# One decode block on one core: maxima by VectorE transposes, softmax sums at the end, wo in 512 columns, and w2 on 112 partitions

## The chip, the core and the metric

The kernel runs on one core of a Trainium2 chip. A core has a matrix engine (TensorE, PE in the profile; its weight loads are listed as PEld), a vector engine (VectorE, DVE), an activation engine (ScalarE, ACT), a general engine (GpSimd, POOL), a queue engine that here issues nearly all transfers (SyncE, SP), and 16 DMA engines that move data between device memory (DRAM) and the core's on-chip memory (SBUF, 128 partitions). Matrix products land in PSUM. The metric is the device time of one execution in microseconds (us).

## The reference

One decode step of a transformer block: the sum of the input, an attention over a cache, and a feed-forward part, both from the same normalised input.

```python
x = A_x                                   # (4, 1, 512), float32 throughout
xn = _layernorm(x)
# attention: 32 heads of 128, cache of 4096 positions for each of 4 batch rows
q = (xn @ wq).reshape(4, 1, 32, 128).transpose(0, 2, 1, 3)
scores = einsum("bhqd,bhkd->bhqk", q, k_cache) * 128 ** -0.5
o = einsum("bhqk,bhkd->bhqd", softmax(scores), v_cache)
a = o.transpose(0, 2, 1, 3).reshape(4, 1, 4096) @ wo        # wo: (4096, 512)
# feed-forward: w1 (512, 1792), w2 (1792, 512)
f = silu(xn @ w1) @ w2
return x + a + f
```

The two caches are 268 MB each; wq and wo are 8.4 MB each, w1 and w2 3.7 MB each. Every byte of them is read once and used for one query row for each batch row.

## The kernel before, in words

**Tiles.** The work on the caches is cut into T = 32 tiles. Tile i holds G = 4 heads of one batch row; its 4 x 4096 cache rows lie as 128 partitions x 128 rows x 128 numbers, so each head has 32 partitions (PH), and a tile of K or V is 128 partitions x 65,536 bytes. K tiles rotate through two buffers, V tiles through one. `load_tile` (line 72) issues each load from SP's queue.

**One turn of the loop (lines 328 to 349).** For tile i: SP issues the load of K tile i+1. VectorE multiplies K by the query in four steps of 32 rows (`products`, L247), GpSimd adds the halves of each row (L251), VectorE sums what is left (`sums`, L262 and L263) into the scores `s`. `maxima` takes the largest score of each partition (L267), and TensorE turns this column into a row (L269). In the next turn `softmax` takes the maximum over each head's 32 partitions (L275), TensorE spreads the four maxima over all partitions (L279), ScalarE copies them with the factor -scale (L281) and takes the exponentials with it as a bias (L285), summing them by partition into `l`. `values` multiplies the exponentials with the V tile on TensorE (L297, 32 matmuls of 512 columns, in four groups of output partitions that run beside each other) into `o_ps`. `heads_out` adds up `l` over each head's partitions with the matrix `same` (L309), copies `o_ps` out (ScalarE, L311), takes the reciprocal of the sum (L315), puts it into the small weights `w_t` (L316), and adds the scaled result into `o_all` (TensorE, L320).

**Order.** Each engine runs its instructions in the order that the tile framework settles from the program; a buffer's reuse is a wait on the engines that last used it. On SP, the load of V tile i waits until `values(i - 1)` has finished, since there is one V buffer, and the load of K tile i+1 stands in the same queue.

**Start (lines 80 to 223).** x, w1, wq and the first K tile are loaded at once. The normalised x is transposed; the hidden row `hp` is computed in four column blocks of 448 (L179), which lie on partitions 0, 32, 64, 96; silu (L185); its result is transposed by 56 small matmuls of 32-column weights (L191) into `hT`, with FC = 14 columns of 128. Then the queries (L206 to L232).

**Tail (lines 352 to 385).** wo is loaded in two pieces into V's buffer and w2 in four pieces (rows 0 to 6, 7 to 10, 11 to 12, 13 of each partition's 14; `W2_CUTS`) into a K buffer, both on 128 partitions. After the last tile, `o_all` is copied (L367), rearranged (L370, L375), and multiplied with wo and w2: `accumulate` (L135) does four matmuls of 128 columns for one row of weights, one for each block of output columns, all added up in `acc`. Then `acc` is copied out (L382) and stored (L385).

Of the kernel before, what the change touches and what calls it, by code (L numbers as in the profile page):

```python
# [1 line left out]

# [14 lines left out]
POOL_ROWS = 32  # L17
POOL_ROWS_LAST = 16
WO_CUTS = (16,)
W2_CUTS = (7, 11, 13)  # L20


@with_exitstack
def kernel(
# [35 lines left out]
    scale = float(Dh) ** -0.5  # L60
# [22 lines left out]
    FJ = F // 4  # L83
# [8 lines left out]

    ident = const.tile([P, P], F32, name="ident")
    make_identity(nc, ident)
    same = const.tile([P, P], F32, name="same")
    nc.gpsimd.memset(same, 0.0)
    for g in range(G):
        nc.gpsimd.memset(
            same[g * PH : (g + 1) * PH, :].rearrange("p (a g) -> p a g", g=G)[:, :, g], 1.0
        )  # L100
    one = const.tile([1, 1], F32, name="one")
    nc.gpsimd.memset(one, 1.0)
# [19 lines left out]
    o_all = ps_1.tile([H, B, Dh], F32, name="o_all")  # L122
    nc.tensor.matmul(
        o_all.rearrange("h b d -> h (b d)"), w_t[:, 0, :H], p_t.rearrange("p r g -> p (r g)"),
        start=True, stop=False,
    )

    pick = const.tile([P, NR * G], F32, name="pick")
# [2 lines left out]
        ident.rearrange("p (j m) -> p m j", j=4)[:, : NR * G, :],  # L131
        axis=AX, op=ALU.add,
    )

    def accumulate(lhsT, rhs, start=False, stop=False):  # L135

        for j in range(D // P):
            nc.tensor.matmul(  # L138
                acc[32 * j : 32 * j + B, :], lhsT, rhs[:, j * P : (j + 1) * P],
                start=start, stop=stop,  # L140
            )
# [28 lines left out]
    xnT = const.tile([P, DC, B], F32, name="xnT")  # L170
# [3 lines left out]


    hp = ps_s.tile([P, FJ], F32, name="sm")
    for c in range(DC):
        for j in range(4):
            nc.tensor.matmul(  # L179
                hp[32 * j : 32 * j + B, :], xnT[:, c, :], w1_t[:, c, j * FJ : (j + 1) * FJ],  # L180
                start=(c == 0), stop=(c == DC - 1),
            )
    for j in range(4):
        rows = slice(32 * j, 32 * j + B)
        nc.scalar.activation(h_sb[rows, :], hp[rows, :], AF.Silu)  # L185
    ht_ps = ps_s.tile([P, FC, B], F32, name="sm")
    h_f = h_sb.rearrange("b (m f) -> b f m", f=FC)
    for f in range(FC):
        for j in range(4):
            rows = slice(32 * j, 32 * j + B)  # L190
            nc.tensor.matmul(  # L191
                ht_ps[32 * j : 32 * j + 32, f, :], h_f[rows, f, :], ident[rows, rows],
                start=True, stop=True,
            )
    hT = const.tile([P, FC, B], F32, name="hT")
    nc.vector.tensor_copy(hT, ht_ps)


    HJ = H // 4
# [1 line left out]
    for hl in range(HJ):  # L201
        for c in range(DC):
            for j in range(4):
                h = HJ * j + hl
                a = PH - B - B * hl
# [4 lines left out]
                    start=(hl == 0 and c == 0),  # L210
                    stop=(hl == HJ - 1 and c == DC - 1),
# [5 lines left out]
    for b in range(B):  # L217
        nc.tensor.matmul(
            qh_ps[:H, b, :], ident.rearrange("p (h b) -> p b h", b=B)[:, b, :], q_all,
            start=True, stop=True,  # L220
# [1 line left out]
    q_h = const.tile([H, B, Dh], F32, name="q_h")  # L222
    nc.vector.tensor_copy(q_h, qh_ps[:H])

    q_ps, vs, st, ls = {}, {}, {}, {}

    def queries(n):

# [12 lines left out]
    def products(i, a):  # L241

        k, q = ks[i], q_ps[i]
        if a == 0:
            st[i] = small.tile([P, R], F32, name="s")
        z = a + STEP
        nc.vector.tensor_tensor(  # L247
            k[:, a:z, :], k[:, a:z, :], q[:, None, :].to_broadcast([P, STEP, Dh]), op=ALU.mult
        )
# [13 lines left out]
        nc.vector.tensor_reduce(s[:, a:v], k[:, a:v, :half], axis=AX, op=ALU.add)  # L263

    def maxima(i):
        m = small.tile([P, 1], F32, name="m")
        nc.vector.tensor_reduce(m, st[i], axis=AX, op=ALU.max)  # L267
        mt = ps_s.tile([1, P], F32, name="sm")
        nc.tensor.transpose(mt, m, ident)  # L269
        return mt  # L270

    def softmax(i, mt):
        s = st.pop(i)
        gm = small.tile([1, G], F32, name="gm", bufs=1)
        nc.vector.tensor_reduce(  # L275
            gm, mt.rearrange("o (g m) -> o g m", g=G), axis=AX, op=ALU.max
        )
        mb = ps_s.tile([P, G], F32, name="sm")
        nc.tensor.matmul(mb, one.to_broadcast([1, P]), gm, start=True, stop=True)  # L279
        nb = small.tile([P, G], F32, name="nb", bufs=1)  # L280
        nc.scalar.activation(nb, mb, AF.Copy, scale=-scale)  # L281
        l = small.tile([P, 1], F32, name="l_t")
        for g in range(G):
            rows = slice(g * PH, (g + 1) * PH)
            nc.scalar.activation(  # L285
                p_t[rows, :, g], s[rows, :], AF.Exp, bias=nb[rows, g : g + 1], scale=scale,
                accum_out=l[rows, :],
            )
        ls[i] = l

    def values(i):
        v, o = vs.pop(i), o_ps
# [12 lines left out]
    def heads_out(i):  # L305

        h, b = i // B * G, i % B
        lt = ps_s.tile([P, 1], F32, name="sm")
        nc.tensor.matmul(lt, same, ls.pop(i), start=True, stop=True)  # L309
        o_sb = small.tile([P, NR, Dh], F32, name="o_sb", bufs=1)  # L310
        nc.scalar.activation(  # L311
            o_sb.rearrange("p r d -> p (r d)"), o_ps, AF.Copy
        )
        rl = small.tile([P, 1], F32, name="rl", bufs=1)
        nc.vector.reciprocal(rl, lt)  # L315
        nc.vector.tensor_scalar_mul(  # L316
            w_t[:, :, W0 : W0 + G], pick.rearrange("p (r g) -> p r g", r=NR), rl
        )
# [8 lines left out]
    mt = None  # L327
    for i in range(T):
        if i > 0 and i + 1 < T:
            ks[i + 1] = load_tile(kpool, "k_t", k_cache, i + 1)  # L330
        products(i, 0)
        if i > 0:
            softmax(i - 1, mt)
# [11 lines left out]
        mt = maxima(i)  # L345
        if i > 0:
            heads_out(i - 1)
        if i % B == 1 and i + B < T:
            queries(i // B + 1)


    wo_t = vpool.tile([P, R, Dh], F32, name="v_t").rearrange("p (c m) d -> p c (m d)", c=H)
    w2_t = kpool.tile([P, R, Dh], F32, name="k_t").rearrange("p r d -> p (r d)")
    w2_t = w2_t[:, : FC * D].rearrange("p (f n) -> p f n", f=FC)
    for t, w, n, cuts in ((wo_t, wo, H, WO_CUTS), (w2_t, w2, FC, W2_CUTS)):
        w = w.rearrange("(p f) n -> p f n", p=P)
        edges = (0, *cuts, n)
        for a, z in zip(edges[:-1], edges[1:]):
            nc.sync.dma_start(t[:, a:z, :], w[:, a:z, :])  # L359

    softmax(T - 1, mt)
# [12 lines left out]
    ot = const.tile([P, H, B], F32, name="ot")  # L374
    nc.vector.tensor_copy(ot, ot_ps.rearrange("p b c -> p c b"))  # L375
# [42 lines left out]
```

## Time and profile before

| | us |
|---|---|
| Median of 3 runs (1310.25 to 1310.54) | 1310.34 |
| The profiled execution's own time | 1310.07 |
| Its span in the profile | 1308.3 |
| VectorE busy | 911.8 |
| GpSimd busy | 511.0 |
| TensorE busy (weight loads 140.7, beside it) | 401.0 |
| ScalarE busy | 97.6 |

The profile shows one execution. "Busy" is the sum of an engine's instructions; the granted clock is the share of TensorE's full clock that it was given, 0.641 in the mean. An fp32 matmul stands in the records as two passes, each with a weight load. In a view by lines, each row is a group of instructions: line, engine, operation, output and inputs with shapes, how many, then busy us and mean ns of one, then the idle time just before them and what ended it. In a timeline or chain, the first two numbers are the start and the duration in us; "issue" is time in which the engine waited for nothing that the profile shows. A view by windows gives busy time of PE, PEld, DVE, ACT and POOL in a stretch, then the granted clock, the busy share of the 16 DMA engines and the GB/s that they moved. In the DMA issues, the last number is the median us from issue to landing.

### The profile page before, as it was taken

What the parts mean: (1) busy time and instruction counts of PE and PEld (TensorE: products, weight loads), DVE (VectorE), ACT (ScalarE), POOL (GpSimd) and SP (SyncE); (2) the same over time, 40 slices, a digit from 0 to 9 for tenths busy, and PEclk for the clock granted to TensorE, in tenths of its full rate; (3) what the DMA queues carried; (4) which work ended last, traced back from release to release, by engine and by line L of the source; (5) the groups of instructions that cost most, each with busy time, mean ns of one, the idle gap of its engine ahead of it and who ended that gap; (6) DMA issues with size and microseconds to landing.
All of it is one profiled execution on the core that took longest, in us unless ns stands there. A gap on an engine that the chain in (4) does not pass through costs nothing.

```text
span 1308.3 us, 7983 instructions
## 1 busy us (share of the span) xinstructions
PE 401.0 (31%) x3326; PEld 140.7 (11%) x3326; DVE 911.8 (70%) x439; ACT 97.6 (7%) x329; POOL 511.0 (39%) x144
## 2 busy tenths in 40 slices
PE   3412333320333322133332133332033333113337
PEld 1301111100111100011110011110011111001114
DVE  1499666787666787666688666678666678766660
ACT  1010000000000000000000000000000000000000
POOL 0255333444332444332444433344433344433340
PEclk7656666655666656666665566665566666566668
DMA  9999999999999999999999999999999999999997
GB/s 401 444 423 440 427 437 432 433 433 433 438 427 437 429 436 429 437 429 437 432 423 443 421 445 425 439 423 441 429 435 427 436 431 433 433 433 433 435 422 327
DMA packets 10443, 561.51 MB, mean 429 GB/s; under 512 B 1172, under 2 KB 1188, under 8 KB 1448
## 3 DMA queue, kind: packets, MB, share of 16 engines
q1 hardware_dynamic: 10392, 561.01, 99.3%
q8 instruction: 26, 0.43, 0.1%
q14 instruction: 9, 0.07, 0.0%
q10 hardware_dynamic: 16, 0.00, 0.0%
HBM read 561.00 MB, written 0.01 MB: 429 GB/s over the span
## 4 chain that ended last, share of the span: by engine, by line
DMA 65%; PE 19%; DVE 12%; POOL 2%; issue 1%; another core or an unknown queue 0%; SPq 0%; POOLq 0%; DVEq 0%
DMA v_t<-in_A_v_cache_dram 39%; DMA k_t<-in_A_k_cache_dram 22%; PE o_ps L297 17%; DVE k_t L247 8%; DVE s L263 3%; DMA k_t<-in_B_w_dram 3%; POOL k_t L251 2%; DMA v_t<-in_A_wq_dram 2%; PE q_ps L232 1%; PE sm L206 1%; DVE s L262 0%; PE sm L269 0%; DVE gm L275 0%; SPq L359 0%
## 5 line engine op out<-in xcount | busy, mean ns | idle before, releaser
L251 POOL TENSOR_TENSOR k_t<-k_t 128x2048 f32<-128x2048 f32 (+1 forms) x128 | 508.5, 3984 | 749.4 <-DVE k_t L247 749.4
L247 DVE TENSOR_TENSOR k_t<-k_t,q_ps 128x4096 f32<-128x4096 f32 x128 | 562.4, 4414 | 246.8 <-DMA k_t<-in_A_k_cache_dram 246.8
L297 PE MATMUL o_ps<-v_t,p_t 128*16 128x512 f32 x1984 | 284.4, 738 | 629.7 <-DMA v_t<-in_A_v_cache_dram 625.9
L263 DVE TENSOR_REDUCE s<-k_t 128x32 f32<-128x2048 f32 (+1 forms) x128 | 257.8, 2014 | 11.2 <-POOL k_t L251 11.2
L297 PEld LDWEIGHTS o_ps<-v_t,p_t 128*16 128x16 f32 x1984 | 65.6, 113 | 836.7 <-issue 832.9
L311 ACT ACTIVATE o_sb<-o_ps 128x512 f32<-128x512 f32 x32 | 19.1, 597 | 1081.3 <-PE o_ps L297 1081.3
L262 DVE TENSOR_REDUCE s<-k_t 128x16 f32<-128x2048 f32 x32 | 72.8, 2276 | 0.0
L232 PE MATMUL q_ps<-q_h,ident 32*32 32x512 f32 x64 | 13.6, 945 | 182.7 <-DVE k_t L247 181.9
L285 ACT ACTIVATE p_t<-s,nb 32x128 f32<-32x128 f32 x128 | 66.0, 516 | 2.7 <-ACT nb L281 0.2
L275 DVE TENSOR_REDUCE gm<-sm 1x4 f32<-1x128 f32 x32 | 8.9, 278 | 53.9 <-PE sm L269 53.9
L320 PE MATMUL o_all<-o_sb,w_t 128*32 128x128 f32 x256 | 34.0, 276 | 2.4 <-ACT o_sb L311 0.7
L320 PEld LDWEIGHTS o_all<-o_sb,w_t 128*32 128x32 f32 x256 | 25.8, 110 | 5.4 <-ACT o_sb L311 1.6
L285 ACT ACTIVATION_READ_ACCUMULATOR p_t<-s,nb 32x1 f32 x128 | 25.0, 196 | 0.0
L232 PEld LDWEIGHTS q_ps<-q_h,ident 32*32 32x32 f32 x64 | 1.6, 127 | 185.2 <-DVE k_t L247 183.5
L269 PE MATMUL sm<-ident,m 128*1 128x128 f32 x32 | 8.9, 277 | 40.4 <-DVE m L267 40.0
L215 DVE COPY q_all<-sm 128x128 f32<-128x128 f32 x1 | 0.3, 292 | 24.4 <-PE sm L206 24.4
L279 PE MATMUL sm<-gm,one 1*128 1x4 f32 x64 | 12.6, 264 | 11.9 <-DVE gm L275 11.7
L206 PE MATMUL sm<-v_t,xpad 128*32 128x128 f32 x256 | 10.5, 342 | 14.1 <-DMA v_t<-in_A_wq_dram 11.2
L375 DVE COPY ot<-sm 128x128 f32<-128x128 f32 x1 | 0.3, 291 | 17.6 <-PE sm L370 17.6
L281 ACT ACTIVATE nb<-sm 128x4 f32<-128x4 f32 x32 | 5.5, 173 | 89.1 <-PE sm L279 89.1
L382 DVE COPY s<-acc 128x128 f32<-128x128 f32 x1 | 0.3, 292 | 16.9 <-PE acc L138 16.9
L206 PEld LDWEIGHTS sm<-v_t,xpad 128*32 128x32 f32 x256 | 9.8, 140 | 14.4 <-issue 14.4
(66 smaller groups left out, 121.9 us busy)
## 6 DMA issues: line engine op xcount, KB each, us to landing
v_t<-in_A_wo_dram SPq DMA_DIRECT2D x2, 4096.0 KB
k_t<-in_B_w_dram SPq DMA_DIRECT2D x1, 3584.0 KB
k_t<-in_B_w_dram SPq DMA_DIRECT2D x1, 1792.0 KB, 32.0
k_t<-in_B_w_dram SPq DMA_DIRECT2D x1, 1024.0 KB, 35.2
k_t<-in_A_k_cache_dram SPq DMA_DIRECT2D x32, 48.8
k_t<-in_B_w_dram SPq DMA_DIRECT2D x1, 512.0 KB, 36.0
v_t<-in_A_v_cache_dram SPq DMA_DIRECT2D x31, 29.6
k_t<-in_B_w_dram SPq DMA_DIRECT2D x1, 256.0 KB
```

The costliest lines, as they stand in the source:

```text
L206: nc.tensor.matmul(qp[32 * j : 32 * j + 32, :], xpad[:, c, a : a + PH], wq_t[:, c, h * Dh : (h + 1) * Dh], start=(hl == 0 and c == 0), sto ...
L232: nc.tensor.matmul(t[g * PH : (g + 1) * PH].rearrange("p b d -> p (b d)"), ident[:H, h : h + 1].to_broadcast([H, PH]), q_h.rearrange("h b ...
L247: nc.vector.tensor_tensor(k[:, a:z, :], k[:, a:z, :], q[:, None, :].to_broadcast([P, STEP, Dh]), op=ALU.mult)
L251: nc.gpsimd.tensor_tensor(k[:, a:v, :half], k[:, a:v, :half], k[:, a:v, half:], op=ALU.add)
L262: nc.vector.tensor_reduce(s[:, v:z], k[:, v:z, :], axis=AX, op=ALU.add)
L263: nc.vector.tensor_reduce(s[:, a:v], k[:, a:v, :half], axis=AX, op=ALU.add)
L269: nc.tensor.transpose(mt, m, ident)
L279: nc.tensor.matmul(mb, one.to_broadcast([1, P]), gm, start=True, stop=True)
L285: nc.scalar.activation(p_t[rows, :, g], s[rows, :], AF.Exp, bias=nb[rows, g : g + 1], scale=scale, accum_out=l[rows, :],)
L297: nc.tensor.matmul(o[j : j + NR * G, :], p_t[:, rows, :].rearrange("p r g -> p (r g)"), v[:, rows, :].rearrange("p r d -> p (r d)"), start ...
L311: nc.scalar.activation(o_sb.rearrange("p r d -> p (r d)"), o_ps, AF.Copy)
L320: nc.tensor.matmul(o_all[:, b, :], w_t[:, r, W0 - h : W0 - h + H], o_sb[:, r, :], start=False, stop=(i == T - 1 and r == NR - 1),)
```

## The change

1. **Maxima.** The column of maxima is put into the first column of a zeroed 128 x 32 tile, and VectorE does the rest: a transpose of 32 x 32 blocks (each head is one block of 32 partitions), a maximum along the row, a multiplication by -scale that also spreads it, and a transpose back. The TensorE transpose, the spreading matmul and ScalarE's copy are gone. The next tile's first product is told to issue after the last of these (`tc.issue_after`).
2. **Sums.** The exponentials' sums go into one tile `l_t` with a column for each tile and head. The sums over partitions, the reciprocals and the scaling are done once, behind the loop; `w_t` is constant.
3. **wo.** One matmul of 512 columns for each row of weights, in four groups of output partitions as in `values`, into a PSUM tile `part`; ScalarE copies it out, and one `accumulate` with `pick` as weights adds the four groups and puts them into `acc`, between the first and the second piece of w2.
4. **silu and w2.** The hidden columns are taken with a step of 4, so that block j of `hp` holds columns 4x + j; `h_sb` is zeroed on all partitions, and 4 matmuls with weights of 112 columns transpose it. hT and w2 then lie on 112 partitions with FC = 16 columns; w2 is loaded in rows 0 to 7, 8 to 11, 12 to 14, 15 of each partition's 16.

Counted in the program, TensorE has 228 matmuls fewer: 96 in the loop, 52 at silu, 96 at wo; 16 are added (8 at w2, 4 with `pick`, 4 for the sums). The matmuls for the sums stand in TensorE's order ahead of the last four tiles' values.

```diff
-W2_CUTS = (7, 11, 13)
+W2_CUTS = (8, 12, 15)
...
-    FC = F // P
+    FJ = F // 4
+    FT = 4
+    FP = FJ // FT
+    FC = F // FP
...
+    nc.gpsimd.memset(h_sb, 0.0)
...
+    l_t = const.tile([P, B, H // G, G], F32, name="l_t")
+    nc.gpsimd.memset(l_t, 0.0)
+    m_t = const.tile([P, PH], F32, name="m_t")
+    nc.gpsimd.memset(m_t, 0.0)
...
+    nc.vector.tensor_copy(w_t[:, :, W0 : W0 + G], pick.rearrange("p (r g) -> p r g", r=NR))
...
+    w1_j = w1_t.rearrange("p c (x j) -> p c j x", j=4)
...
-                hp[32 * j : 32 * j + B, :], xnT[:, c, :], w1_t[:, c, j * FJ : (j + 1) * FJ],
+                hp[32 * j : 32 * j + B, :], xnT[:, c, :], w1_j[:, c, j, :],
...
-    ht_ps = ps_s.tile([P, FC, B], F32, name="sm")
-    h_f = h_sb.rearrange("b (m f) -> b f m", f=FC)
-    for f in range(FC):
-        for j in range(4):
-            rows = slice(32 * j, 32 * j + B)
-            nc.tensor.matmul(
-                ht_ps[32 * j : 32 * j + 32, f, :], h_f[rows, f, :], ident[rows, rows],
-                start=True, stop=True,
-            )
+    ht_ps = ps_s.tile([FP, FT, 4, B], F32, name="sm")
+    h_t = h_sb.rearrange("k (p t) -> k t p", t=FT)
+    for t in range(FT):
+        nc.tensor.matmul(
+            ht_ps[:, t], h_t[:, t, :], ident.rearrange("p (j m) -> p j m", j=4)[:, :, :B],
+            start=True, stop=True,
+        )
...
     def maxima(i):
-        m = small.tile([P, 1], F32, name="m")
-        nc.vector.tensor_reduce(m, st[i], axis=AX, op=ALU.max)
-        mt = ps_s.tile([1, P], F32, name="sm")
-        nc.tensor.transpose(mt, m, ident)
-        return mt
+        nc.vector.tensor_reduce(m_t[:, :1], st[i], axis=AX, op=ALU.max)
+        mt = small.tile([P, PH], F32, name="mt", bufs=1)
+        nc.vector.transpose(mt, m_t)
+        gm = small.tile([P, 1], F32, name="gm", bufs=1)
+        nc.vector.tensor_reduce(gm, mt, axis=AX, op=ALU.max)
+        mb = small.tile([P, PH], F32, name="mb", bufs=1)
+        nc.vector.tensor_scalar_mul(mb, gm.to_broadcast([P, PH]), -scale)
+        nb = small.tile([P, PH], F32, name="nb", bufs=1)
+        return nb, nc.vector.transpose(nb, mb).ins
...
-                p_t[rows, :, g], s[rows, :], AF.Exp, bias=nb[rows, g : g + 1], scale=scale,
-                accum_out=l[rows, :],
+                p_t[rows, :, g], s[rows, :], AF.Exp, bias=nb[rows, :1], scale=scale,
+                accum_out=l_t[rows, i % B, i // B, g : g + 1],
...
-        products(i, 0)
+        with tc.issue_after(done) if i > 0 else nullcontext():
+            products(i, 0)
...
-    w2_t = w2_t[:, : FC * D].rearrange("p (f n) -> p f n", f=FC)
+    w2_t = w2_t[:FP, : FC * D].rearrange("p (f n) -> p f n", f=FC)
...
-        w = w.rearrange("(p f) n -> p f n", p=P)
+        w = w.rearrange("(p f) n -> p f n", f=n)
...
+    ls_ps = ps_s.tile([H, B], F32, name="sm")
+    for b in range(B):
+        nc.tensor.matmul(
+            ls_ps[:, b : b + 1], l_t[:, b].rearrange("p n g -> p (n g)"), ones,
+            start=True, stop=True,
+        )
+    rl = const.tile([H, B], F32, name="rl")
+    nc.vector.reciprocal(rl, ls_ps)
...
-    nc.scalar.activation(o_row, o_all, AF.Copy)
+    nc.vector.tensor_tensor(
+        o_row, o_all, rl[:, :, None].to_broadcast([H, B, Dh]), op=ALU.mult
+    )
...
+    part = ps_q.tile([P, D], F32, name="q_ps")
+    nc.vector.memset(part, 0.0)
     for c in range(H):
-        accumulate(ot[:, c, :], wo_t[:, c, :])
-    for f in range(FC):
+        j = 32 * (c % 4)
+        nc.tensor.matmul(
+            part[j : j + B, :], ot[:, c, :], wo_t[:, c, :], start=(c < 4), stop=(c >= H - 4)
+        )
+    part_sb = small.tile([P, D], F32, name="o_sb", bufs=1)
+    nc.scalar.activation(part_sb, part, AF.Copy)
+    for f in range(W2_CUTS[0]):
+        accumulate(hT[:, f, :], w2_t[:, f, :])
+    accumulate(pick[:, :B], part_sb)
+    for f in range(W2_CUTS[0], FC):
         accumulate(hT[:, f, :], w2_t[:, f, :], stop=(f == FC - 1))
```

More of the change, by code (lines that the diff above doesn't have):

```diff
@@ L1 @@
-from contextlib import ExitStack
+from contextlib import ExitStack, nullcontext
 import concourse.bass as bass
@@ L82 @@
     NP = 2 * PH - B
-    FJ = F // 4
     h_sb = scratch[:, 4 * D : 4 * D + FJ]
@@ L94 @@
     make_identity(nc, ident)
[L95 to L99, printed above, removed]
-        )
-    one = const.tile([1, 1], F32, name="one")
-    nc.gpsimd.memset(one, 1.0)
+    ones = const.tile([P, 1], F32, name="ones")
+    nc.gpsimd.memset(ones, 1.0)
+    nc.gpsimd.memset(h_sb, 0.0)
     nc.vector.memset(xpad, 0.0)
@@ L185 @@
         nc.scalar.activation(h_sb[rows, :], hp[rows, :], AF.Silu)
-    ht_ps = ps_s.tile([P, FC, B], F32, name="sm")
-    h_f = h_sb.rearrange("b (m f) -> b f m", f=FC)
-    for f in range(FC):
-        for j in range(4):
-            rows = slice(32 * j, 32 * j + B)
-            nc.tensor.matmul(
-                ht_ps[32 * j : 32 * j + 32, f, :], h_f[rows, f, :], ident[rows, rows],
-                start=True, stop=True,
-            )
-    hT = const.tile([P, FC, B], F32, name="hT")
-    nc.vector.tensor_copy(hT, ht_ps)
+    ht_ps = ps_s.tile([FP, FT, 4, B], F32, name="sm")
[5 more added lines that the diff above has]
+        )
+    hT = const.tile([FP, FC, B], F32, name="hT")
+    nc.vector.tensor_copy(hT, ht_ps.rearrange("p t j b -> p (t j) b"))
     HJ = H // 4
@@ L223 @@
     nc.vector.tensor_copy(q_h, qh_ps[:H])
-    q_ps, vs, st, ls = {}, {}, {}, {}
+    q_ps, vs, st = {}, {}, {}
     def queries(n):
@@ L265, in maxima, with softmax @@
     def maxima(i):
-        m = small.tile([P, 1], F32, name="m")
-        nc.vector.tensor_reduce(m, st[i], axis=AX, op=ALU.max)
-        mt = ps_s.tile([1, P], F32, name="sm")
-        nc.tensor.transpose(mt, m, ident)
-        return mt
-    def softmax(i, mt):
-        s = st.pop(i)
[L274 to L282, printed above, removed]
+        nc.vector.tensor_reduce(m_t[:, :1], st[i], axis=AX, op=ALU.max)
[7 more added lines that the diff above has]
+        return nb, nc.vector.transpose(nb, mb).ins
+    def softmax(i, nb):
+        s = st.pop(i)
         for g in range(G):
@@ L307, in heads_out @@
         h, b = i // B * G, i % B
-        lt = ps_s.tile([P, 1], F32, name="sm")
-        nc.tensor.matmul(lt, same, ls.pop(i), start=True, stop=True)
         o_sb = small.tile([P, NR, Dh], F32, name="o_sb", bufs=1)
@@ L312, in heads_out @@
             o_sb.rearrange("p r d -> p (r d)"), o_ps, AF.Copy
[L313 to L317, printed above, removed]
         )
@@ L326 @@
     ks[1] = load_tile(kpool, "k_t", k_cache, 1)
-    mt = None
+    nb = done = None
     for i in range(T):
@@ L330 @@
             ks[i + 1] = load_tile(kpool, "k_t", k_cache, i + 1)
-        products(i, 0)
+        with tc.issue_after(done) if i > 0 else nullcontext():
+            products(i, 0)
         if i > 0:
-            softmax(i - 1, mt)
+            softmax(i - 1, nb)
         if i > 0:
@@ L344 @@
         del ks[i], q_ps[i]
-        mt = maxima(i)
+        nb, done = maxima(i)
         if i > 0:
@@ L359 @@
             nc.sync.dma_start(t[:, a:z, :], w[:, a:z, :])
-    softmax(T - 1, mt)
+    softmax(T - 1, nb)
     values(T - 1)
     heads_out(T - 1)
+    ls_ps = ps_s.tile([H, B], F32, name="sm")
[6 more added lines that the diff above has]
+    nc.vector.reciprocal(rl, ls_ps)
     o_row = const.tile([H, B, Dh], F32, name="o_row")
-    nc.scalar.activation(o_row, o_all, AF.Copy)
+    nc.vector.tensor_tensor(
+        o_row, o_all, rl[:, :, None].to_broadcast([H, B, Dh]), op=ALU.mult
+    )
     ot_ps = ps_s.tile([P, B, H], F32, name="sm")
```

1 line of the change is left out of this document (removed).

## The prediction

> **What bounds the kernel now.** I read the page from the top: busy times, slices, queues.
>
> ```profile
> span 1308.3 us, 7983 instructions
> PE 401.0 (31%) x3326; PEld 140.7 (11%) x3326; DVE 911.8 (70%) x439; ACT 97.6 (7%) x329; POOL 511.0 (39%) x144
> ...
> DMA  9999999999999999999999999999999999999997
> ...
> q1 hardware_dynamic: 10392, 561.01, 99.3%
> q8 instruction: 26, 0.43, 0.1%
> ```
>
> No compute engine is above 70%, while the 16 DMA engines are at 90% or more in all slices but the last; the load queue alone fills 99.3% of their time. 561 MB have to come in. The stages, by windows:
>
> ```profile
> 100.00:1200.00 1100.00, 321.98 (x2245) 102.07 (x2237) 802.54 (x373) 82.33 (x290) 447.50 (x114) 0.63 1.00 433
> ...
> 1298.00:1300.00 2.00, 1.36 (x48) 0.83 (x36) 0.00 (x0) 0.00 (x0) 0.00 (x0) 1.00 0.87 340
> 1300.00:1302.00 2.00, 0.91 (x28) 0.54 (x24) 0.00 (x0) 0.00 (x0) 0.00 (x0) 1.00 0.54 219
> 1302.00:1304.00 2.00, 1.18 (x38) 0.87 (x41) 0.00 (x0) 0.00 (x0) 0.00 (x0) 1.00 0.24 86
> ```
>
> The last three columns are granted clock, DMA share and GB/s. The loop moves 433 GB/s at a share of 1.00, so a tile of 128 x 65,536 bytes (8.39 MB) takes 19.4 us, and each turn loads two. Only at the very end does the share fall: from 1298 on, some DMA engines have finished and a few (0.24 x 16, about four) still work in 1302 to 1304. The slowest engine sets the end. The chain of waits says the same:
>
> ```profile
> 1178.54 9.46 PE o_ps L297 x64
> 1188.00 0.06 PE sm L269
> 1188.06 29.07 DMA v_t<-in_A_v_cache_dram
> ...
> 1267.84 35.99 DMA k_t<-in_B_w_dram
> 1303.84 0.04 issue
> 1303.88 0.62 PE acc L138 x16
> 1304.53 0.45 PE acc L138 x8
> 1305.02 0.04 issue
> 1305.07 0.29 DVE s L382
> ```
>
> TensorE stands in this chain with some 9 us a turn (the values' product frees the V buffer for the next load), but that is no loss. The issues:
>
> ```profile
> k_t<-in_A_k_cache_dram SPq DMA_DIRECT2D x32, 48.8
> v_t<-in_A_v_cache_dram SPq DMA_DIRECT2D x31, 29.6
> ```
>
> A V load lands 29.6 us after its issue, and 19.4 of these are its own transfer. So 10.2 us of K are still ahead of it when it is issued; it could be issued that much later before an engine ran dry.
>
> **The change, part by part.** The loop first: maxima, softmax, heads_out.
>
> ```profile
> L247 DVE TENSOR_TENSOR k_t<-k_t,q_ps 128x4096 f32<-128x4096 f32 x128 | 562.4, 4414 | 246.8 <-DMA k_t<-in_A_k_cache_dram 246.8
> ...
> L267 DVE TENSOR_REDUCE m<-s 128x1 f32<-128x128 f32 x32 | 9.2, 286 | 1.1
> L275 DVE TENSOR_REDUCE gm<-sm 1x4 f32<-1x128 f32 x32 | 8.9, 278 | 53.9 <-PE sm L269 53.9
> ...
> L316 DVE TENSOR_SCALAR w_t<-pick,rl 128x16 f32<-128x16 f32 x32 | 7.5, 234 | 1.1
> ...
> L315 DVE RECIPROCAL rl<-sm 128x1 f32<-128x1 f32 x32 | 4.7, 146 | 3.0 <-PE sm L309 3.0
> ...
> L223 DVE COPY q_h<-q_ps 32x512 f32<-32x512 f32 x1 | 0.7, 679 | 1.3 <-PE q_ps L218 1.3
> ```
>
> VectorE loses 0.278 + 0.146 + 0.234 = 0.66 us a tile and gains two transposes, a reduction and a multiplication, all 128 x 32. The trace has no VectorE transpose; its nearest small rows are 0.146 and 0.679 us. I take 0.234 each, being nearest in shape: 4 x 0.234 - 0.66 = +0.28 us a tile, at most +2.1. VectorE idles 246.8/31 = 8.0 us a tile waiting for K, so this costs nothing; without that cover it would be 32 x 0.28 = 9 us. The issue_after keeps the next tile's first product behind the transposes; what queues there is SP's release of K buffers, and K has its 48.8 - 19.4 = 29 us. A relief, worth nothing here: VectorE no longer waits for TensorE (53.9 us in total), since the maximum no longer goes through TensorE's queue behind the values. ScalarE loses the nb copy; its exponentials now wait for each other, for they write one l_t. Four of some 0.5 us with a wait between them still end well ahead of V, most narrowly at the last tile:
>
> ```profile
> 1268.83 0.51 ACT L285 ACTIVATE p_t<-s,nb 32x128 f32<-32x128 f32 x1
> ...
> 1275.26 8.89 PE L297 MATMUL o_ps<-k_t,p_t 128*16 128x512 f32 x64 [5.47 <-DMA k_t<-in_A_v_cache_dram]
> ```
>
> That is 5.5 us of cover. Loop: 0.
>
> Start: 56 small transposes of silu's result become 4, and w1 is read with a step of 4 elements.
>
> ```profile
> 12.32 5.02 PE L179 MATMUL sm<-k_t,xnT 128*4 128x448 f32 x32 [4.68 <-DMA k_t<-in_B_w_dram]
> ...
> 32.78 7.26 PE L206 MATMUL sm<-v_t,xpad 128*32 128x128 f32 x192 [11.18 <-DMA v_t<-in_A_wq_dram]
> ...
> 48.49 2.00 PE L232 MATMUL q_ps<-q_h,ident 32*32 32x512 f32 x16 [0.77 <-DVE q_h L223]
> ...
> 52.22 8.75 DVE L247 TENSOR_TENSOR k_t<-k_t,q_ps 128x4096 f32<-128x4096 f32 x2 [3.78 <-DMA k_t<-in_A_k_cache_dram]
> ```
>
> TensorE waits for wq until 32.78 whatever comes before, so the removed transposes bring nothing. The stepped reading is not in the trace: between 5.0 us as now and, at a quarter of the rate, 20 us. Even that, with silu behind it, ends near 36, makes the queries 3 us late (53.5 for 50.5) and VectorE's first tile 1.3 us late, against the 10 us (V) and 29 us (K) by which loads are issued ahead. Start: 0. [...]
>
> Instruction fetches: 6,652 TensorE records and 0.43 MB on q8 make 65 bytes a record, so q8 carries TensorE's program, on the same DMA engines as the data. Removed matmuls: 3 x 32 in the loop, 52 at silu, 96 at wo; added 8 + 4 + 4: 228 fewer, of 4 records each, 14%, or 3.6 of 26 packets. A share of 0.1% (0.05 to 0.15) of 16 x 1308.3 us is 0.4 to 1.2 us a packet: 1.4 to 4.3 us of engine time, spread over 16 engines 0.1 to 0.3 us. I take -0.2; none if the slowest engine fetched nothing, up to -4.3 if it fetched all of them.
>
> Tail: wo, the sums, w2.
>
> ```profile
> 1288.21 5.34 PE L138 MATMUL acc<-v_t,ot 128*4 128x128 f32 x128 [0.38 <-DVE ot L375]
> ...
> 1294.69 3.68 PE L138 MATMUL acc<-v_t,ot 128*4 128x128 f32 x128 [1.14 <-DMA v_t<-in_A_wo_dram]
> ...
> 1299.01 1.06 PE L138 MATMUL acc<-k_t,hT 128*4 128x128 f32 x32 [0.64 <-DMA k_t<-in_B_w_dram]
> ...
> 1300.70 0.84 PE L138 MATMUL acc<-k_t,hT 128*4 128x128 f32 x24 [0.64 <-issue]
> ...
> 1302.59 1.06 PE L138 MATMUL acc<-k_t,hT 128*4 128x128 f32 x32 [1.05 <-DMA k_t<-in_B_w_dram]
> ```
>
> wo's 32 matmuls of 512 columns have the form of the values (8.89 us for 32): 4.4 us a half instead of 5.34 and 3.68. The first half would end at 1292.7, before the second lands; the second at 1299.1, as w2's first piece arrives. The sums (four one-column matmuls, a reciprocal of 0.15) leave the loop for places before the last values; the scaled o_row, now on VectorE, costs some 0.68 us (q_h's copy, of its shape), ahead of a wait of 2 us. w2's first 8 rows and the added pick row are 72 records where 56 were: 16 more at 0.84/24 = 0.035, 0.6 us, inside the 1.05 us wait before 1302.59. So TensorE's savings fall into waits for DMA. The last piece is still one row; the one before has three rows, not two (24 records, 0.84, for 16, 0.62), and the last may start 0.1 late: +0.1. If the clock had dropped to half by then, these last two pieces would take twice as long, 0.84 + 0.45 = 1.3 us more.
>
> w2's load: the same 3.67 MB, 8.5 us at 433 GB/s, but on 112 partitions. No row has a large load on fewer than 128. Bounds: 0, if 16 engines take 7 rows each at full rate; if the way into SBUF is divided by partitions, 112 of 128 give 7/8 of the rate, 9.7 us, +1.2; and if engines meet on one way half of the time, 8.5 x 1.5 = 12.7, +4.2. I take +0.6, between the first two: the loop's 433 GB/s at a DMA share of 1.00 say that there the engines bind, and these would be as evenly loaded with 7 rows as with 8. [...]
>
> Sum, against the profiled execution's own 1310.07 us (span 1308.3 and 1.8 around; the median of the runs shown, 1310.34, is 0.3 above): 0 + 0 - 0.2 + 0.1 + 0.6 = +0.5, so **1310.6 us**.
>
> **The rivals.**
> w2's load stretched by engines that meet in SBUF: +4.2 - 0.2 + 0.1 gives 1314.2, slower. For it: nothing is behind w2 to hide it, and the four late engines of 1302 to 1304 show that one late engine moves the end. Against it: no row with such a meeting. It is decided at +2.5 us on the last landing, 30% of w2's transfer.
> The loop starves (a V load issued over 10.2 us later, or VectorE over 8 us longer a tile, by transposes of 4 us): each us beyond the cover costs 32 us, or in the first turns alone some 3: 1313 upward. Nothing in the rows is near it.
> The fetches were what made the last engines late: -2.9 (middle of 1.4 to 4.3) gives 1307.2, faster. Against it: about four engines are late, and one engine's relief leaves the others.
> A cold TensorE at the tail: 1310.6 + 1.3 = 1311.9. For it: a wait of some 2 us in mid-wo; against: granted clock 1.00 from 1298 on.
> That fewer instructions mean no time at all is the forecast itself.
>
> **How the numbers follow.** Forecast (w2 between 0 and +1.2) 0.57, own range 1309.4 to 1311.6; cold tail 0.05; meeting in SBUF 0.29, of which 0.03 stays within 0.2%; starving 0.04; fetches 0.05. A measurement of this kernel can tell some 0.2%, 2.6 us, from no change: slower 0.26 + 0.04 = 0.30, faster 0.05, same 0.65. The range, 1309.2 to 1314.4, takes in the forecast, the cold tail and most of the stretched load; left out are the fetches and the far ends above.
>
> **What would show it.** The loop's DMA share stays at 1.00 and 433 GB/s; V lands some 29.6 us after issue; q8 shows 22 or 23 packets; idle time of VectorE before L249 stays with K's DMA; TensorE's records fall to about 2,870. wo's two halves end before w2's first piece lands. The last landing of w2 stays at 1304.5 to 1305.5; at 1307 or later, with a longer stretch of low DMA share, the first rival is right. A loop share under 0.99, or SP waiting for VectorE, would make the forecast wrong.

## The result, and the profile after

The changed kernel takes 1318.7 us in the median (1317.35 to 1319.51), the kernel before 1310.43 on the same chip: a ratio of 1.0059, with a 95% interval of 1.0048 to 1.0070. It is slower by 8.3 us; 1310.6 was forecast, with a range up to 1314.4. The profiled execution took 1318.97 us, with a span of 1316.1: 7.8 us more span than before.

The page of the changed kernel first. Its rows answer to the busy times, slices and queues of before; the last two are DMA issues (w2's third piece and the V loads), with KB and us from issue to landing.

```profile
span 1316.1 us, 7057 instructions
PE 377.8 (29%) x2902; PEld 114.4 (9%) x2902; DVE 919.7 (70%) x475; ACT 92.2 (7%) x297; POOL 511.0 (39%) x142
...
DMA  9999999999999999999999999999999999999997
GB/s 399 443 437 427 435 428 437 431 433 434 434 429 437 426 439 432 430 435 432 425 441 431 433 435 426 435 437 430 436 425 440 429 434 429 435 436 426 437 423 226
...
q8 instruction: 22, 0.36, 0.1%
...
L249 DVE TENSOR_TENSOR k_t<-k_t,q_ps 128x4096 f32<-128x4096 f32 x128 | 562.3, 4414 | 288.7 <-DMA k_t<-in_A_k_cache_dram 288.6
...
k_t<-in_B_w_dram SPq DMA_DIRECT2D x1, 672.0 KB, 44.5
...
v_t<-in_A_v_cache_dram SPq DMA_DIRECT2D x31, 29.5
```

TensorE has 424 records fewer (2,902; about 2,870 were forecast, and a few records can be missing from a trace), q8 four packets fewer, and a V load lands 29.5 us after its issue, as before. The DMA digits are the same 9s. Only the GB/s show where the time is: from the second slice on all lie between 423 and 443, and the last at 226. The windows of the changed kernel (busy time of PE, PEld, DVE, ACT, POOL, then granted clock, DMA share, GB/s) put a border on it:

```profile
100.00:1200.00 1100.00, 297.49 (x2080) 83.12 (x2076) 810.33 (x403) 77.38 (x261) 448.84 (x114) 0.63 1.00 433
1294.00:1296.00 2.00, 0.00 (x0) 0.00 (x0) 0.00 (x0) 0.00 (x0) 0.00 (x0) 1.00 1.02 229
...
1298.00:1300.00 2.00, 2.00 (x13) 0.30 (x9) 0.00 (x0) 0.00 (x0) 0.00 (x0) 0.50 0.92 180
...
1308.00:1310.00 2.00, 1.41 (x32) 0.65 (x28) 0.00 (x0) 0.00 (x0) 0.00 (x0) 0.50 0.49 178
1310.00:1312.00 2.00, 2.00 (x44) 1.25 (x40) 0.00 (x0) 0.00 (x0) 0.00 (x0) 0.50 0.04 15
```

The loop is what it was: 433 GB/s at a share of 1.00. Once w2 comes in on 112 partitions, all engines are still busy (a share of 1.02 is 1.00: in so short a stretch, transfers that end behind its border count in full) and move 229 GB/s, 0.53 of the loop's rate. The timeline and the chain of waits of the changed kernel show what follows:

```profile
1288.59 3.62 PE L382 MATMUL q_ps<-v_t,ot 128*4 128x512 f32 x32 [0.38 <-DVE ot L376]
...
1297.48 4.90 PE L382 MATMUL q_ps<-v_t,ot 128*4 128x512 f32 x32 [5.28 <-DMA v_t<-in_A_wo_dram]
...
1309.15 1.39 PEld L141 LDWEIGHTS acc<-k_t,hT 112*4 112x4 f32 x32 [1.09 <-DMA k_t<-in_B_w_dram]
1309.16 3.59 PE L141 MATMUL acc<-k_t,hT 112*4 112x128 f32 x64 [0.59 <-DMA k_t<-in_B_w_dram]
1310.83 1.42 PEld L141 LDWEIGHTS acc<-k_t,hT 112*4 112x4 f32 x32 [0.29 <-DMA k_t<-in_B_w_dram]
```

```profile
1265.85 43.26 DMA k_t<-in_B_w_dram
...
1309.16 3.64 PE acc L141 x64
...
1312.82 0.29 DVE s L394
```

w2's second piece lands at 1309.1; its third is what the weight loads at 1310.83 wait for. Before, the third landed at 1303.83 (the end of the 35.99 us in the chain shown in the prediction) and `acc` was copied at 1305.07, 1.24 us later. Now it is 1310.8 and 1312.82, 2.0 us. So of 7.8 us of span, 7.0 are w2's later landing and 0.8 are TensorE between the landing and the copy, at a granted clock of 0.50.

The single transfers say it too. In the trace's DMA records a 16-KB transfer of w2 takes 1.20 us in the median; on 128 partitions, in experiment 4 below, one of the same size takes 0.61.

### The profile page after: what moved, and what is told of

It reads as the page before. It is cut to its first block, busy times and chain, and to the rows that moved or that the text cites. A ratio compares the mean times of both kernels' runs of the same rounds, so it can differ in the third digit from the quotient of the medians.

```text
span 1316.1 us, 7057 instructions
## 1 busy us (share of the span) xinstructions
PE 377.8 (29%) x2902; PEld 114.4 (9%) x2902; DVE 919.7 (70%) x475; ACT 92.2 (7%) x297; POOL 511.0 (39%) x142
## 4 chain that ended last, share of the span: by engine, by line
DMA 62%; DVE 19%; PE 13%; POOL 4%; issue 1%; another core or an unknown queue 1%; SPq 0%; ACT 0%; POOLq 0%; DVEq 0%; ACTq 0%
DMA k_t<-in_A_k_cache_dram 35%; DMA v_t<-in_A_v_cache_dram 22%; DVE k_t L249 12%; PE o_ps L294 11%; DVE s L265 6%; POOL k_t L253 4%; DMA k_t<-in_B_w_dram 3%; DMA v_t<-in_A_wq_dram 2%; DVE s L264 1%; PE q_ps L234 1%; PE sm L208 1%; PE acc L141 0%; SPq L79 0%; DVE m_t L269 0%
## 5 line engine op out<-in xcount | busy, mean ns | idle before, releaser
L249 DVE TENSOR_TENSOR k_t<-k_t,q_ps 128x4096 f32<-128x4096 f32 x128 | 562.3, 4414 | 288.7 <-DMA k_t<-in_A_k_cache_dram 288.6
L294 PE MATMUL o_ps<-k_t,p_t 128*16 128x512 f32 x64 | 9.3, 747 | 7.2 <-DMA k_t<-in_A_v_cache_dram 7.2
L382 PE MATMUL q_ps<-v_t,ot 128*4 128x512 f32 x64 | 8.5, 681 | 5.7 <-DMA v_t<-in_A_wo_dram 5.3
L269 DVE TENSOR_REDUCE m_t<-s 128x1 f32<-128x128 f32 x32 | 9.1, 285 | 1.1
## 6 DMA issues: line engine op xcount, KB each, us to landing
k_t<-in_B_w_dram SPq DMA_DIRECT2D x1, 672.0 KB, 44.5
v_t<-in_A_v_cache_dram SPq DMA_DIRECT2D x31, 29.5
```

Of the source, the lines that this page charges most:

```text
L249: nc.vector.tensor_tensor(k[:, a:z, :], k[:, a:z, :], q[:, None, :].to_broadcast([P, STEP, Dh]), op=ALU.mult)
L269: nc.vector.tensor_reduce(m_t[:, :1], st[i], axis=AX, op=ALU.max)
L294: nc.tensor.matmul(o[j : j + NR * G, :], p_t[:, rows, :].rearrange("p r g -> p (r g)"), v[:, rows, :].rearrange("p r d -> p (r d)"), start ...
L382: nc.tensor.matmul(part[j : j + B, :], ot[:, c, :], wo_t[:, c, :], start=(c < 4), stop=(c >= H - 4))
```

## The experiments

My theory after the result: w2's load on 112 partitions goes at about half rate, and this alone makes the kernel slower. Rivals: the other parts (loop, wo in 512 columns) carry a share; TensorE's lower clock at the end does; it is w2's four pieces and 16 rows, their step in DRAM, or the deal of rows to engines, and not the partitions.

**1. The change without its fourth part.** silu and w2 as before (56 small transposes, w2 on 128 partitions), all else changed.

```diff
-W2_CUTS = (8, 12, 15)
+W2_CUTS = (7, 11, 13)
...
-    FC = F // FP
+    FC = F // P
...
-    w2_t = w2_t[:FP, : FC * D].rearrange("p (f n) -> p f n", f=FC)
+    w2_t = w2_t[:, : FC * D].rearrange("p (f n) -> p f n", f=FC)
...
```

> The changed kernel with its fourth part undone: silu's 56 small transposes, hT and w2 on 128 partitions with 14 rows each, as before; maxima, sums and wo stay changed. Theory (the DMA engines meet in SBUF when w2 is written on 112 partitions): the last piece of w2 lands near 1304.5 us again, the stretch at a DMA share near 1 and half the GB/s is gone, 1309.6 to 1310.6 us in all. Rival (wo in 512 columns, or the loop, does the harm, w2 only shows it): still 1315 us or more.

Measured: 1308.85 us (1308.41 to 1310.0), ratio to the kernel before 0.9989 (0.9980 to 0.9998). Windows, then chain, of this kernel:

```profile
100.00:1200.00 1100.00, 301.12 (x2088) 83.68 (x2080) 809.37 (x403) 77.36 (x261) 448.82 (x114) 0.63 1.00 433
1290.00:1300.00 10.00, 7.52 (x80) 1.80 (x76) 0.00 (x0) 0.60 (x1) 0.00 (x0) 1.00 0.91 381
1302.00:1304.00 2.00, 1.74 (x52) 1.14 (x56) 0.00 (x0) 0.00 (x0) 0.00 (x0) 1.00 0.09 36
```

```profile
1267.61 35.63 DMA k_t<-in_B_w_dram
...
1303.29 0.62 PE acc L138 x16
```

w2's third piece lands at 1303.24, as early as before, 35.6 us after its issue; with 112 partitions it took 44.5. Parts 1 to 3 are no loss: with w2 left alone the kernel is 1.5 us faster than before, and beats both.

**2. The fourth part alone**, on the kernel before.

```diff
-W2_CUTS = (7, 11, 13)
+W2_CUTS = (8, 12, 15)
...
+    w1_j = w1_t.rearrange("p c (x j) -> p c j x", j=4)
...
+    w2_t = w2_t[:FP, : FC * D].rearrange("p (f n) -> p f n", f=FC)
...
```

> The kernel before with the fourth part alone: w1 taken in steps of 4, silu's result transposed by 4 matmuls, w2 on 112 partitions with 16 rows each. Theory (meeting in SBUF): 1316 to 1319 us, the packets of w2 take about twice their time. Rival (wo or the loop does the harm): 1310 to 1311 us.

Measured: 1317.82 us (1317.1 to 1318.58), ratio 1.0056 (1.0042 to 1.0070). A window and the chain:

```profile
1290.00:1306.00 16.00, 8.57 (x208) 6.17 (x196) 0.00 (x0) 0.00 (x0) 0.00 (x0) 0.79 0.94 197
```

```profile
1265.39 41.08 DMA k_t<-in_B_w_dram
...
1307.45 5.29 PE acc L141 x120
```

One part alone makes 7.5 of the 8.3 us, and the times of this kernel and of the changed one overlap. In this window, the last of wo and most of w2 come in at 197 GB/s. Together with the first run this settles which part it was.

**3. w2 on 64 partitions**, 28 rows each. If the partitions decide, the same bytes on fewer of them show it again.

```diff
-W2_CUTS = (8, 12, 15)
+W2_CUTS = (14, 21, 26)
...
-    FT = 4
+    FT = 7
```

> The changed kernel with w2 on 64 partitions and 28 rows each (silu's result transposed by 7 matmuls with weights of 64 columns); the same bytes. Theory (fewer partitions reach fewer ways into SBUF, and engines meet there): half the rate or worse, 8.5 us of w2 become 17, the last landing 1309 to 1314 us, in all 1316 to 1322. Rival (a row step of 32 KB in DRAM, or 7 rows an engine, is what slows the load): with a step of 56 KB and 4 rows an engine it goes at full rate, 1310 to 1312 us.

Measured: 1323.15 us (1322.37 to 1326.19), ratio 1.0101 (1.0087 to 1.0115). First a window of the changed kernel, then the same window and a row of the chain of this one:

```profile
1290.00:1306.00 16.00, 7.41 (x68) 1.48 (x60) 0.00 (x0) 0.60 (x1) 0.00 (x0) 0.89 0.99 228
```

```profile
1290.00:1306.00 16.00, 8.59 (x52) 1.37 (x44) 0.00 (x0) 0.60 (x1) 0.00 (x0) 0.72 0.96 196
```

```profile
1307.05 10.84 PE acc L141 x232
```

196 GB/s, 0.45 of the 433 of the changed kernel's loop, where 112 partitions had 228 in the changed kernel and 197 in experiment 2, so 64 are hardly worse than 112. The step from row to row in DRAM is not the cause: it is 32 KB in the changed kernel and 56 KB here, both slow, and 64 KB in experiment 4 below, which is fast. The rest of the time is TensorE, which with 28 rows to multiply for 16 runs late at the low clock (0.50 from 1310 on; 10.84 us).

**4 and 5. The same pieces on 128 and on 96 partitions.** The rows are taken from wo's memory, in the changed kernel's pieces of 8, 4, 3 and 1 rows a partition; w2 is left out of the computation. The bytes differ (4.19 and 3.15 MB for 3.67). Dealt evenly, 96 partitions are six rows for each of 16 engines, an even number where 112 are seven.

```diff
+    w2_all = w2_t[:, : FC * D].rearrange("p (f n) -> p f n", f=FC)
+    w2_t = w2_all[:96]
...
+        if n == FC:
+            w = wo.rearrange("(p f) n -> p f n", f=H)
+            t = w2_all
...
+            nc.sync.dma_start(t[:(P if n == H else 96), a:z, :], w[:(P if n == H else 96), a:z, :])
...
```

> The changed kernel, but its w2 tile is loaded from wo's memory in place of w2: the same four pieces of 8, 4, 3 and 1 rows of 2 KB, on 128 partitions instead of 112 (the matmuls still use 112 of them, and the last product is one with wrong weights; w2 is left out). 4.19 MB instead of 3.67. Theory (112 partitions make the engines meet): full rate again, 9.7 us of load, 1.2 us more than the kernel with w2's 14 rows on 128 partitions (1308.85), so 1309.5 to 1310.6. Rival (the pieces, their sizes, the product with pick in between or the 4-matmul transpose): 1316 or more.

> As the run with 128 partitions of wo's memory, but on 96 partitions (6 rows for each of 16 engines, 3.15 MB; the matmuls use 96, and the last product is one with wrong weights; w2 is left out). Theory (any load on fewer than 128 partitions lets engines meet): about half the rate, 14.5 us in place of 7.3, 1313 to 1319 us. Rival (only an odd number of rows for an engine, as 7, is slow): 1307.5 to 1308.5 us.

Measured: on 128 partitions 1310.49 us (1310.06 to 1312.86), ratio 1.0003 (0.9993 to 1.0012); on 96 1316.42 us (1315.1 to 1316.66), ratio 1.0043 (1.0028 to 1.0058). A window and a row of the chain of each, 128 first:

```profile
1290.00:1300.00 10.00, 7.09 (x76) 1.68 (x70) 0.00 (x0) 0.60 (x1) 0.00 (x0) 0.93 0.98 409
```

```profile
1267.07 36.74 DMA k_t<-in_A_wo_dram
```

```profile
1290.00:1304.00 14.00, 8.03 (x52) 1.43 (x48) 0.00 (x0) 0.00 (x0) 0.00 (x0) 0.76 0.99 219
```

```profile
1266.56 42.40 DMA k_t<-in_A_wo_dram
```

A quarter fewer bytes land 5.2 us later (1308.96 for 1303.81), at 219 GB/s for 409, from the same memory with the same pieces. So neither the pieces nor w2's place in memory are the cause, nor an odd number of rows for an engine: what changed between the two is the number of partitions, and with it, if they are dealt evenly, the rows for an engine (six for eight). By the DMA records a 16-KB transfer takes 1.19 us with 96 partitions, for 0.61 with 128.

**6 and 7. The clock at the end.** Matmuls whose result nobody uses are put between wo and w2, to keep TensorE busy while it waits.

```diff
...
+    junk = ps_s.tile([P, D], F32, name="sm")
+    for c in range(12):
+        j = 32 * (c % 4)
+        nc.tensor.matmul(
+            junk[j : j + B, :], ot[:, c, :], wo_t[:, H - 1, :], start=True, stop=True
+        )
...
```

The first try had 8 of them in one output group.

> The changed kernel with 8 more matmuls of 512 columns behind wo, into a PSUM tile that nobody reads, so that TensorE does not idle for 3 us before w2's first piece. Theory (of the 8 us, some 1.3 are the half clock under which the last two pieces of w2 are worked off): granted clock 1.00 to the end, 0.6 to 0.8 us from the last landing to the copy of acc instead of 2.0, 1317.4 us. Rival (all of the loss is the DMA): 1318.7 us as without them.

> The changed kernel with 12 more matmuls of 512 columns behind wo in four groups of output partitions, some 2.6 us in all, into a PSUM tile that nobody reads; eight of them one behind the other had taken 6.6 us and made TensorE late. Theory (some 1.3 of the 8 us are the half clock of the last two pieces): clock 1.00 to the end, 1317.4 us. Rival (all of the loss is the DMA): 1318.7 us.

The first gave 1320.15 us (1319.88 to 1320.57) and says nothing: one group kept TensorE for 6.60 us, until 1310.7, so that TensorE and no longer the load came last. The second, above, took 2.75 us and gave 1317.71 (1317.27 to 1319.71), ratio 1.0059 (1.0042 to 1.0076). First a row of the timeline of the first try, then a window and the chain of the second:

```profile
1304.08 6.60 PE L387 MATMUL sm<-v_t,ot 128*4 128x512 f32 x15
```

```profile
1308.00:1310.00 2.00, 0.77 (x30) 0.46 (x25) 0.00 (x0) 0.00 (x0) 0.00 (x0) 1.00 0.57 207
```

```profile
1267.24 44.15 DMA k_t<-in_B_w_dram
...
1311.44 1.10 PE acc L141 x32
...
1312.56 0.29 DVE s L400
```

The clock was 1.00 from 1304 on, and from landing (1311.39) to copy it is 1.2 us again, where the changed kernel needs 2.0. So the low clock is worth 0.8 us in the profiles; between the medians it is 1.0 us, with ranges that overlap. It follows from w2's late rows, for which TensorE waits idle (0.50 from 1308 on behind those waits, 1.00 with the added matmuls ahead of them), and is no cause of its own.

**8 and 9. What the removed instructions were worth.** The first run's kernel gets 64 more matmuls of 4 columns a turn, so that TensorE's program is longer. At the first try they read only constants; at the second, whose edit is shown, they read each tile's `o_sb`.

```diff
...
+        if i < T - 1:
+            junk = ps_s.tile([P, 4], F32, name="sm")
+            for n in range(64):
+                nc.tensor.matmul(junk[:4], o_sb[:, 0, :4], o_sb[:, 0, :4], start=True, stop=True)
```

> The kernel with parts 1 to 3 of the change and w2 on 128 partitions (1308.85 us), and 64 tiny matmuls (4 columns) more in 31 turns of the loop, where TensorE waits for V: 1,984 matmuls, 7,936 records, 31 more packets of instructions on q8. Theory (the gain of 1.5 us over the kernel before comes from fewer instruction fetches on the DMA engines; a packet holds an engine some 1.2 us): 31 x 1.2 / 16 = 2.3 us more, and up to twice that if the slowest engine gets more than its share: 1311 to 1313.5 us. Rival (fetches cost nothing that can be seen; the gain is in the loop or at wo): 1308.5 to 1309.3 us.

> The kernel with w2 on 128 partitions, and behind each tile's output (o_sb) 64 more matmuls of 4 columns that read o_sb and whose result nobody uses: 1,984 in all, some 7,900 records more, spread over the loop. They stand behind the matmuls that free V's buffer, so they hold nothing back. Theory 1 (TensorE's program costs load time, since it comes over the same 16 DMA engines): the instruction queue goes from 23 packets to about 54; the trace gives such a packet about 1.07 us of an engine and 0.5 us more for the packet behind it, so 31 more cost between 31 x 1.07 / 16 = 2.1 and 31 x 1.57 / 16 = 3.0 us: 1311.0 to 1311.9. Rival (these fetches fall into slack, or the last engine isn't the one that fetched): 1308.9 within 0.6. Either way a loop at a DMA share of 1.00; GB/s 433 by the rival, about 432 by theory 1.

The first failed as a test: 1402.26 us. Nothing tied the matmuls to their turns, all 1,984 were put ahead of the first values, TensorE kept V's buffer (SP's longest wait for it was 106.6 us), and the loads ran dry:

```profile
DMA  9990039999999999999999999999999999999997
GB/s 403 442 427 40 5 122 448 420 422 446 424 442 427 439 425 441 426 440 426 438 429 435 433 435 434 433 429 438 429 436 422 440 427 438 427 442 425 441 424 338
```

The second gave 1314.99 us (1314.81 to 1316.29), 6.1 more than without the extra matmuls. A queue, a window, SP's waits (us in total, times, longest) and a row of the chain of this kernel:

```profile
q8 instruction: 54, 0.88, 0.3%
```

```profile
100.00:1200.00 1100.00, 387.04 (x5784) 179.18 (x5784) 807.98 (x402) 77.46 (x261) 448.98 (x114) 0.63 1.00 431
```

```profile
SPq L77 <- DMA v_t<-in_A_v_cache_dram: 812.1, 30, 30.7
SPq L77 <- PE o_ps L292: 304.0, 30, 14.5
```

```profile
1272.45 37.34 DMA k_t<-in_B_w_dram
```

q8 has 31 packets more (54 for 23). The loop moves 431 GB/s for 433 at the same share of 1.00, and w2's third piece is issued 4.8 us later. SP waits for TensorE 304.0 us in total, no longer than without the extra matmuls (310.5), and for V's data 812.1 instead of 803.3, so it is not that TensorE starved the loads. 6.1 us over 31 packets are 0.20 us a packet, two to three times what I had expected. The DMA records account for most of what the loop lost: between 100 and 1200 this kernel brings in 31 data packets of 64 KB fewer, 4.7 us at 433 GB/s. Its 29 more instruction packets hold the engines 30.7 us longer, and its data packets, usually 2.42 us each, together some 28 us; over 16 engines the two are 3.7 us, and the instruction packets' own time is about half of that. That they also delay the data packets, and not another effect of 7,900 more records, is the likeliest reading, but this run can't part the two.

**10. wo back in 128 columns**, on the first run's kernel: only the loop's parts 1 and 2 are left of the change.

```diff
...
     for c in range(H):
-        nc.tensor.matmul(
-            part[j : j + B, :], ot[:, c, :], wo_t[:, c, :], start=(c < 4), stop=(c >= H - 4)
-        )
+        accumulate(ot[:, c, :], wo_t[:, c, :])
...
```

> The kernel with w2 on 128 partitions, and wo back in 128 matmuls of 128 columns instead of 32 of 512: what is left of the change is the loop (VectorE transposes, the sums at the end). It tells where the 1.5 us by which that kernel beats the kernel before come from. Theory 1 (the tail: TensorE done earlier with wo): 1310.3, the gain is gone, with TensorE ending later after the last landing. Theory 2 (fewer instruction fetches): some 88 matmuls more, 350 records or 1.4 packets: 1309.0. Rival (the loop as such, its earlier issues): 1308.9, the gain stays.

Measured: 1309.66 us (1308.56 to 1310.88), ratio 0.9993 (0.9984 to 1.0002), with 24 packets on q8. That lies between what was expected if the gain came from the tail (1310.3) and what the other two readings gave (1309.0 and 1308.9). Its range overlaps both kernels', and the interval includes no change at all. If a packet is worth 0.20 us, the three that the first run's kernel has fewer than before (23 for 26) are 0.6 us of its gain of 1.5, and this run's two are 0.4 of its 0.7. Where the rest comes from stays open.

**11 and 12. Where the rows land.** If engines meet on a way into SBUF, rows placed otherwise might keep them apart. Each piece of w2 comes in seven loads of 16 rows, to partitions 8e+k (gaps zeroed) or, as a control, to 7e+k.

```diff
-            nc.sync.dma_start(t[:, a:z, :], w[:, a:z, :])
+                for k in range(7):
+                    nc.sync.dma_start(
+                        t.rearrange("(e k) f n -> k e f n", k=8)[k, :, a:z, :],
+                        w.rearrange("(e k) f n -> k e f n", k=7)[k, :, a:z, :],
+                    )
...
```

> The changed kernel with w2's load dealt anew: each piece comes as seven loads of 16 rows, and row 7e+k goes to partition 8e+k (e 0 to 15, k 0 to 6), so that 112 of 128 partitions are filled with a gap at every eighth; the gaps are zeroed beforehand by VectorE and their rows of hT are zero. Bytes, rows in memory and matmuls are those of the changed kernel. Theory 1 (it is where the rows land in SBUF: the 112 contiguous rows make engines meet on one way in, and eight-partition groups keep them apart): w2 at 433 GB/s again, 1309 to 1311. Rival (any load of other than 128 rows, or of 3.67 MB in this form, is at half rate whatever partitions it goes to; or 28 loads cost more each): 1318 or later.

> The same seven loads of 16 rows a piece and the same zeroing, but row 7e+k goes to partition 7e+k, as in the changed kernel: 112 contiguous partitions. Between this and the kernel with rows 8 apart only the partitions differ. Theory 1 (where the rows land): 1318 to 1320, as the changed kernel. Rival (it is the form of the single load of 112 rows, not the partitions): 1309 to 1311, as the other.

Measured: 1323.54 us (1320.87 to 1324.93) with rows 8 apart, 1322.47 (1322.03 to 1322.94) with rows 7 apart. A window of each, 8 apart first, and two rows of the latter's chain:

```profile
1290.00:1306.00 16.00, 10.35 (x60) 1.73 (x52) 0.00 (x0) 0.60 (x1) 0.00 (x0) 0.70 0.83 205
```

```profile
1290.00:1306.00 16.00, 11.71 (x72) 2.06 (x68) 0.00 (x0) 0.60 (x1) 0.00 (x0) 0.68 0.87 220
```

```profile
1305.57 0.51 SPq L355
...
1314.57 2.07 DMA k_t<-in_B_w_dram
```

Both are slower still, since the form costs time of its own: SP stood until 1305.57 before it could issue the last loads, and then issued them one by one. But the window holds mostly the large first pieces, and they came in at 205 and 220 GB/s, at DMA shares of 0.83 and 0.87. With all engines busy that would be 247 and 253, still little over half of 433. So this placement is no cure, and neither is a load of 16 rows, one for each engine if they are dealt evenly. The control was faster by 7%, and by 2% where both are taken with all engines busy. But several of these loads are under way at once, so the comparison isn't a clean one. So it stays open by what mechanism fewer than 128 partitions lose half of the rate.

## Why the prediction was wrong

**The step that failed** is w2's load: "I take +0.6, between the first two: the loop's 433 GB/s at a DMA share of 1.00 say that there the engines bind". The load lost 7.0 us. A share of 1.00 says that the engines are busy, not what they are busy with: with 112 partitions they were as busy (1.02) at 229 GB/s. The loop's rows could not tell engines that are the limit themselves from engines that something else holds up, because every large load in the trace was on 128 partitions; what the limit is on 112, no run here shows. The upper bound was too low as well. That engines meet on one way half of the time, 1.5 times as long, was a guess with no row behind it; at 229 GB/s w2's 3.67 MB take 16.0 us for 8.5, 1.9 times as long. That the way into SBUF is divided by partitions (7/8 of the rate, +1.2) was an estimate too, and no run shows it: the rate was 0.53 of the loop's on 112 partitions and 0.45 on 64.

**The first rival** (engines that meet, 1314.2, chance 0.29) was right that the last landing would be the sign: 2.5 us later was to decide for it, and it came 7.0 later, after 1307. It expected a longer stretch of low DMA share with it; there the share was 0.99 over 1290 to 1306, and the rate was half (228 GB/s for 433). Its size was 4.2 where the trace shows 7.0. And that it is a meeting of engines in SBUF is not shown; the runs show a half rate and not why.

**The cold TensorE** came. The tail's term for TensorE was +0.1, and it cost 0.8 us where 1.3 was worked out for half clock (0.50 was granted). The wait in mid-wo that was named grew to 5.3 us, and the clock was 0.50 in 1298 to 1300 behind it; but that stood under w2's load, and the clock was back at 1.00 in 1302 to 1304. What counted was 0.50 from 1308 on, behind the waits for w2. The clock of 1.00 that spoke against this rival belonged to a tail with short waits, of 1.1 us and less.

**What held.** Loop: +0.28 us of VectorE a tile was forecast; the four new groups of the changed kernel are

```profile
L271 DVE STREAM_TRANSPOSE mt<-m_t 128x32 f32<-128x32 f32 x32 | 6.8, 212 | 1.1
L277 DVE STREAM_TRANSPOSE nb<-mb 128x32 f32<-128x32 f32 x32 | 6.8, 211 | 3.3
...
L273 DVE TENSOR_REDUCE gm<-mt 128x1 f32<-128x32 f32 x32 | 6.0, 186 | 1.1
L275 DVE TENSOR_SCALAR mb<-gm 128x32 f32<-128x32 f32 x32 | 5.8, 181 | 1.1
```

0.79 us for the 0.66 removed, +0.13, and idle time before L249 is K's DMA alone. Start: w1 read with a step takes 6.47 us for 5.02, near the lower end of the bounds, and TensorE still waits for wq afterwards:

```profile
12.79 6.47 PE L183 MATMUL sm<-k_t,xnT 128*4 128x448 f32 x32 [3.24 <-DMA k_t<-in_B_w_dram]
...
32.15 7.22 PE L208 MATMUL sm<-v_t,xpad 128*32 128x128 f32 x168 [7.43 <-DMA v_t<-in_A_wq_dram]
```

Fetches: 22 packets, as forecast; -0.2 us was probably too little, 4 packets at 0.20 being 0.8. wo: its first half ends at 1292.2 (1292.7 forecast), its second at 1302.4 instead of 1299.1, because its rows land at 1297.48 and not 1294.69 and it ran at the low clock at first (0.50 in 1298 to 1300; 4.90 us for the first half's 3.62). As I read it, the engines that are done with wo first begin w2, and what they do there slows the others: 18 of wo's 256 transfers of 32 KB took over 1.5 us, where the median is 1.22, and none did before. That is hidden behind w2. The sum is then 7.0 + 0.8 for the 7.8 us of span; the gains of parts 1 to 3, 1.5 us without part 4, can't be told apart beside it. One sum of the prediction was inconsistent: the time for the rival on fetches, 1307.2, leaves out the +0.6 and +0.1 that the forecast counts; with them it is 1307.9. Nothing hangs on it.

## What to carry to other kernels

In a kernel that waits for loads, saving instructions on an idle engine is worth little (parts 1 to 3: 1.5 us here), while the shape of a load is worth much (7.0 us): keep loads that nothing hides on all 128 partitions, even if a matmul would like 112. A busy share of 1.00 of the DMA engines is no proof of full rate (1.02 at 229 GB/s here); read GB/s beside it, and treat a load of a shape that the trace doesn't have as unknown up to some twice its time (here 196 to 229 GB/s for 433).

## What the runs showed that was not expected

With the DMA engines at a share of 0.94 to 1.02, loads ran at 197 to 229 GB/s on 112 partitions, at 219 on 96 and at 196 on 64; on 128 they ran at 409 to 433, at a share of 0.98 to 1.00. An instruction queue that takes 0.1% to 0.3% of the DMA engines' time by the page seems to cost more than that: 31 packets more went with 6.1 us, 0.5% of the run. And the tail that waited longer for its loads ran at half TensorE clock (0.50 from 1308, where the kernel before kept 1.00), so the late rows were paid once more when they arrived.
